# Hash attention and a maxout FFN on one core: the last third of `w_out` is loaded with the middle third, into the tiles that stage the output

## The chip, the cores and the metric

One core of a Trainium2 chip runs the whole program. The metric is device time in microseconds (us) from the start to the end of the program, the median of several runs; lower is better. A profile of a single execution gives the times inside.

## The reference

```
# q, k, v: (4, 8, 768, 64) float32   proj: (64, 6)   w1, w2, w3: (512, 768)   w_out: (768, 512)
q_bits, k_bits = (q @ proj > 0), (k @ proj > 0)      # 6 bits give a bucket for each position
mask   = bucket(q)[:, None] == bucket(k)[None, :]
scores = where(mask, (q @ k.T) / sqrt(64), -1e9)
attn   = softmax(scores)                             # per batch and head, 768 x 768
x      = (attn @ v), heads side by side              # (3072, 512)
h      = max(max(x @ w1, x @ w2), x @ w3)            # (3072, 768)
out    = h @ w_out                                   # (3072, 512)
```

## The kernel before

The work is cut by batch `b` (4), by pair of heads `pr` (4) and by half of the query positions `hf` (2). For each pair, q, k and v are loaded in float32 (`load`, L250), split on VectorE and ScalarE into two float16 parts (`split_h` L268 or L266, `split_r` L273), and turned so that the head dimension lies on the partitions. For the first six pairs TensorE turns them (`pe_T`, L292), for the others a transposing DMA from SyncE (`xbar`, L282, tile `T`). TensorE multiplies the operands with the hash matrix (`hash_mm`, L312); VectorE makes the bits, TensorE turns them, and two small DMAs bring them through DRAM into the operand's spare rows (`bit_out` L349, `bit_in` L352). A score (`score`, L395) then has the hash match in it, and `expo` (L401, ScalarE) makes the weights `AT`. `attend` (L413) multiplies them with v and sums into one PSUM tile `av`; there is a single `av` buffer, which VectorE frees by `norm_t` (L430). GpSimd sums v for the mean (`vsum`, L363 to L366), TensorE spreads it (`mean_mm`, L376), and ScalarE casts v (`vcast`, L202, tile `vone`).

When all four pairs of a half are done, `x` is turned by a DMA (`x_bar`, L457, tile `xT`) and the FFN of that half (`ffn`) is spread between the scores of the next one: `l1` (L478) multiplies by w1, w2 and w3, `l1_evac` takes the maximum (L487), `l2` (L496) multiplies by `wout_sb`, ScalarE copies the result out of PSUM into a tile `osb` (`l2_evac`, L202; pool `op`, `OSB` = 5 buffers), and SyncE stores it (`store`, L507).

The order on each engine is fixed before the program runs. `Plan.run` goes through a table of tasks with planned costs, priorities and counted buffers, and calls each task's function when the plan would start it; on the chip an engine works through its own list in that order and only waits for semaphores. So all DMAs that SyncE issues stand in one list, and an instruction that waits holds up all behind it. Each of them uses one of eight DMA semaphores in turn, so it also waits for the DMA issued eight before it.

The weights come from `weights(b, pr, parts)`. Half of `w3`, and `w_out` in three thirds, are loaded in float32 by SyncE into a staging tile `ws` (`stage_w`, L670; two buffers of 1024 elements a partition) and cast to float16 by GpSimd (`cast_w`, L204 through `copy`). A third of `w_out` is two blocks of 128 rows, 512 KB. With two `ws` buffers the third load waits until the first cast is done. The plan has a task for each load and each cast:

```
ld = add(("SP", 0.5), -60 if w == "o" else -70, [], lambda e, w=w, i=i: stage_w(w, i, e), take=("ws",),
         xfer=1.4 if w == "o" else 1.1, after=[prev])
...
parts.append(add(("POOL", 1.5 if w == "o" else 1.1), -60, [ld], lambda e, w=w, i=i: cast_w(w, i, e),
                 give=("ws",)))
```

The pair whose loads follow the first two thirds on SyncE's list is (2, 0): batch 2, pair 0. Behind them stand the transposing DMA of pair (1, 3), then the third load, then the `x_bar` of batch 0's second half.

Of the kernel before, what the change touches and what calls it, by code (L numbers as in the profile page):

```python
# [8 lines left out]
FP32 = mybir.dt.float32  # L9
# [124 lines left out]
def kernel(  # L134
# [12 lines left out]
    nc = tc.nc  # L147
    B, H, S, D = q.shape
    NBITS = proj.shape[1]
    P = 128  # L150
    NCH = S // P
    DM = H * D
# [34 lines left out]
    op = ctx.enter_context(tc.tile_pool(name="op", bufs=OSB))  # L187
# [12 lines left out]
    def copy(e, o, i):  # L200
        if e == "ACT":
            nc.scalar.copy(o, i)  # L202
        else:
            ENG[e].tensor_copy(o, i)  # L204
# [21 lines left out]
    wout_sb = konst.tile([P, NF, DM], FP16, name="wout_sb")  # L226
# [430 lines left out]
    wst_tiles = {}  # L657

    def w_view(w, i):
        c = slice(2 * i, 2 * i + 2)  # L660
        if w == "o":
            return moe_w_out.rearrange("(c p) m -> p c m", p=P)[:, c, :], wout_sb[:, c, :]
        f = slice(w[0] * DF // 2, (w[0] + 1) * DF // 2)
        return (moe_w1, moe_w2, moe_w3)[w[1]].rearrange("(c p) f -> p c f", p=P)[:, c, f], w_sb[w[1]][:, c, f]

    def stage_w(w, i, e):
        from_dram = w_view(w, i)[0]
        t = wst.tile([P, 2 * DM], FP32, tag="ws", name="ws")
        wst_tiles[w, i] = t[:, 0 : 2 * from_dram.shape[2]].rearrange("p (c f) -> p c f", c=2)
        nc.sync.dma_start(wst_tiles[w, i], from_dram)  # L670

    def cast_w(w, i, e):
        copy(e, w_view(w, i)[1], wst_tiles.pop((w, i)))

    def weights(b, pr, parts):
        if (pr or b) and parts[0] not in plain and parts[0] != "o":
            prev = add(("POOL", 0.1), -150, [bounced[b, pr]], lambda e: hold(b, pr, e), after=[wprev[0]])
        elif pr or b:
            prev = bounced[b, pr]
        else:  # L680
            prev = ready_v[0, 0]
        for w in parts:
            if w == "o" or w in plain:
                parts = []
                for i in range(NF // 2) if w == "o" else range(NJ // 2):
                    ld = add(("SP", 0.5), -60 if w == "o" else -70, [], lambda e, w=w, i=i: stage_w(w, i, e), take=("ws",),
                             xfer=1.4 if w == "o" else 1.1, after=[prev])
                    prev = ld
                    parts.append(add(("POOL", 1.5 if w == "o" else 1.1), -60, [ld], lambda e, w=w, i=i: cast_w(w, i, e),
                                     give=("ws",)))  # L690
                wload[w] = plan.join(parts, ())
                continue
            else:
                prev = add(("POOL", 0.8), -100, [], lambda e, w=w: None if w == LATE else load_w(w[1], w[0], e),
                           xfer=2.15, after=[prev])
            wload[w] = prev
        wprev[0] = prev
# [116 lines left out]
```

## Time and profile before

| what | us |
|---|---|
| median of five runs | 268.29 |
| the five runs | 265.15, 265.61, 268.29, 268.84, 268.96 |
| the profiled execution, its own time | 267.9 |
| its span, first to last instruction | 266.1 |
| TensorE busy | 256.6 (96% of the span) |
| ScalarE busy | 196.2 (74%) |
| VectorE busy | 177.0 (67%) |
| GpSimd busy | 41.8 (16%) |
| granted TensorE clock | 0.999 of full speed |

The profiled execution's own time is 1.8 us longer than its span. Times within the profile count from the span's start. In the profile's lines the columns of the timeline are start, duration, engine, line, operation, output and inputs, the count of instructions merged, and in brackets the idle time before and what ended it. SPq is SyncE's list; a DMA's duration there is the time to issue it, not to move its bytes. KB and MB are as the profile counts them.

### The profile page before, as it was taken

How to read it: one execution, taken by the hardware profiler on the slowest of the kernel's cores; microseconds unless marked ns; L12 is line 12 of the kernel's file. 1: busy time of each engine (PE TensorE's matmuls, PEld its weight loads, DVE VectorE, ACT ScalarE, POOL GpSimd, SP SyncE). 2: the span in 40 equal slices, each digit the busy share in tenths (PEclk: the TensorE clock that was granted, in tenths of full speed). 3: DMA queues.
4: the chain of work that ended last, by engine and by line, in shares of the span. 5: the costliest groups of instructions: out<-in, count | busy, mean ns of one | idle time of the engine just before them, and what ended most of it. 6: DMA issues, size and time to landing. Idle time of an engine off the chain costs nothing.

```text
span 266.1 us, 7323 instructions
## 1 busy us (share of the span) xinstructions
PE 256.6 (96%) x2992; PEld 174.8 (66%) x2992; DVE 177.0 (67%) x394; ACT 196.2 (74%) x283; POOL 41.8 (16%) x57
## 2 busy tenths in 40 slices
PE   8599999999999999999999999999999999999995
PEld 8488776767656666677666767765666656565552
DVE  4699789989857898458985795651655526345260
ACT  5589999987936889989989889898899642332422
POOL 1331056083310333003330030000000000000000
PEclk9999999999999999999999999999999999999999
DMA  6991489999997899979993997312030060120303
GB/s 188 336 288 36 137 257 268 282 229 331 228 231 244 219 274 167 221 224 205 182 286 109 217 166 132 61 22 84 36 62 0 4 173 6 42 79 0 121 0 119
DMA packets 67408, 41.69 MB, mean 157 GB/s; under 512 B 48046, under 2 KB 63662, under 8 KB 67374
## 3 DMA queue, kind: packets, MB, share of 16 engines
q1 hardware_dynamic: 64654, 39.26, 57.7%
q0 software_dynamic: 2640, 1.97, 4.8%
q8 instruction: 23, 0.38, 0.6%
q14 instruction: 11, 0.09, 0.1%
q10 hardware_dynamic: 80, 0.00, 0.0%
HBM read 25.72 MB, written 6.84 MB: 122 GB/s over the span
## 4 chain that ended last, share of the span: by engine, by line
PE 79%; DMA 9%; DVE 4%; ACT 2%; SPq 2%; POOL 1%; issue 1%; ACTq 0%; POOLq 0%
PE ps L478 32%; PE sc L395 19%; PE po L496 11%; PE av L413 10%; DMA v<-in_v_dram 2%; PE hps L312 2%; DMA q<-in_q_dram 2%; DMA dr<-bt 2%; DMA ws<-in_moe_w_dram 2%; PE tps L292 2%; ACT AT L401 2%; DVE s L273 1%; SPq L250 1%; DVE s L268 1%; PE hps L310 1%
## 5 line engine op out<-in xcount | busy, mean ns | idle before, releaser
L401 ACT ACTIVATE AT<-sc 128x768 f16<-128x768 f32 x192 | 146.2, 815 | 14.9 <-PE sc L395 12.9
L478 PE MATMUL ps<-xT,w_sb 128*128 128x384 f16 x576 | 106.3, 326 | 0.0
L395 PE MATMUL sc<-T 128*128 128x384 f16 x384 | 92.9, 325 | 1.0 <-ACT AT L401 0.4
L487 DVE TENSOR_TENSOR ht<-ht,ps 128x384 f16<-128x384 f16 x96 | 52.9, 551 | 47.1 <-PE ps L478 44.7
L413 PEld LDWEIGHTS <-AT 128*128 128x128 f16 x1152 | 59.5, 97 | 22.8 <-issue 0.2
L478 PEld LDWEIGHTS <-w_sb 128*128 128x128 f16 x576 | 52.6, 98 | 30.4 <-issue 0.5
L413 PE MATMUL av<-vone,AT 128*128 128x65 f16 x1152 | 65.5, 193 | 0.0
L395 PEld LDWEIGHTS <-T 128*128 128x128 f16 x384 | 30.3, 97 | 11.8 <-issue 1.5
L496 PE MATMUL po<-wout_sb,ht 128*128 128x512 f16 (+1 forms) x150 | 33.7, 370 | 0.0
L202 ACT CAST ht<-ps 128x384 f16<-128x384 f32 x28 | 13.4, 479 | 26.2 <-DVE ht L487 19.1
L202 ACT COPY osb<-po 128x512 f32<-128x512 f32 (+1 forms) x24 | 13.6, 568 | 18.6 <-PE po L496 18.6
L273 DVE SCALAR_TENSOR_TENSOR s<-q,s 128x384 f16<-128x384 f32 x32 | 21.8, 697 | 4.6 <-ACT s L266 4.4
L363 POOL TENSOR_TENSOR vt<-v 128x384 f32<-128x384 f32 x12 | 14.1, 1179 | 66.9 <-DMA v<-in_v_dram 66.7
L430 DVE TENSOR_TENSOR t<-av,mv 128x390 f32<-128x390 f32 x32 | 17.9, 561 | 7.9 <-PE av L413 7.8
L496 PEld LDWEIGHTS <-ht 128*128 128x128 f16 x150 | 14.1, 98 | 13.7
L449 DVE TENSOR_TENSOR xn<-t,rr 128x384 f16<-128x384 f32 x32 | 19.0, 592 | 1.1
L273 DVE SCALAR_TENSOR_TENSOR s<-k,s 128x384 f16<-128x384 f32 x32 | 18.8, 606 | 0.2
L204 DVE CAST ht<-ps 128x384 f16<-128x384 f32 x20 | 11.1, 555 | 10.5 <-PE ps L478 10.2
L292 PE MATMUL tps<-iden,s 128*128 128x128 f16 x168 | 13.7, 223 | 2.6 <-DVE bit L322 2.4
L292 PEld LDWEIGHTS <-s 128*128 128x128 f16 x168 | 11.0, 100 | 3.9 <-DVE s L273 2.7
L202 ACT CAST vone<-v 128x768 f16<-128x768 f32 x12 | 10.0, 836 | 1.4 <-DMA v<-in_v_dram 1.4
L312 PEld LDWEIGHTS <-T 128*128 128x128 f16 x336 | 10.0, 96 | 1.0
(54 smaller groups left out, 142.3 us busy)
## 6 DMA issues: line engine op xcount, KB each, us to landing
v<-in_v_dram SPq DMA_DIRECT2D x16, 384.0 KB
out_dram<-osb SPq DMA_DIRECT2D x23, 256.0 KB
q<-in_q_dram SPq DMA_DIRECT2D x15, 384.0 KB
k<-in_k_dram SPq DMA_DIRECT2D x15, 384.0 KB
w_sb<-in_moe_w_dram POOLq DMA_DIRECT2D x5, 384.0 KB, 11.6
ws<-in_moe_w_out_dram SPq DMA_DIRECT2D x3, 512.0 KB
ws<-in_moe_w_dram SPq DMA_DIRECT2D x2, 384.0 KB
dr<-bt SPq DMA_DIRECT2D x15, 36.0 KB
```

The costliest lines, as they stand in the source:

```text
L202: nc.scalar.copy(o, i)
L273: nc.vector.scalar_tensor_tensor(out=s[:, a0:a1, D : 2 * D], in0=raw_view(n, b, pr, heads), scalar=QS, in1=s[:, a0:a1, 0:D], op0=AluOp.mul ...
L292: nc.tensor.transpose(p16[:, c * P : (c + 1) * P], S16[b, pr][:, a0 + c, :], iden[:])
L312: nc.tensor.matmul(o, T[b, pr][:, a, :], PAB[:], start=True, stop=True)
L395: nc.tensor.matmul(sc[:, i, 0:HQ], t[:, NA2 + hh * NCH + 2 * j + i, :], t[:, hh * NCH + hf * CH : hh * NCH + (hf + 1) * CH, :], start=True ...
L401: nc.scalar.activation(AT[:], scs.pop(u)[:, :, 0:HQ], ActFn.Exp, bias=EXP_BIAS, scale=EXP_SCALE)
L413: nc.tensor.matmul(av[:, o : o + D + 1], AT[:, i, c * P : (c + 1) * P], vones[b % 2][:, 2 * pr + hh, 2 * j + i, 0 : D + 1], start=slot == ...
L430: nc.vector.tensor_tensor(out=t[:, :, :, 0 : D + 1], in0=av[:, :, :, 0 : D + 1], in1=mv, op=AluOp.add)
L449: nc.vector.tensor_tensor(out=xv, in0=t[:, :, :, 0:D], in1=rr[:].to_broadcast([P, 2, CH, D]), op=AluOp.mult)
L478: nc.tensor.matmul(ps[:, 0:HQ], w_sb[i][:, jc, fb * P : (fb + 1) * P], xTs[b, hf][:, jc, :], start=jc == 0, stop=jc == NJ - 1)
L487: nc.vector.tensor_tensor(out=ht[:], in0=ht[:], in1=ps[:, 0:HQ], op=AluOp.max)
L496: nc.tensor.matmul(ps[:, m0:m1], hts[b, hf, fb][:, c * P : (c + 1) * P], wout_sb[:, fb, m0:m1], start=fb == 0, stop=fb == NF - 1)
```

## The change

The last third (blocks 4 and 5 of `w_out`, 256 KB each) is no longer loaded into a `ws` tile by a task of its own. When the plan reaches the load of the middle third, `stage_w` first issues two loads into two tiles of the output staging pool `op` (tag `osb`), and then the middle third's load into `ws`. When it reaches the middle third's cast, GpSimd casts the two blocks first and then the middle third. The tasks of the last third stay in the plan with their planned costs, and emit nothing. The plan's count of free `osb` buffers is not changed by the two tiles.

```diff
     def stage_w(w, i, e):
+        if w == "o" and i == 2:
+            return
+        if w == "o" and i == 1:
+            for c in (4, 5):
+                wst_tiles[w, c] = op.tile([P, DM], FP32, tag="osb", name="osb")
+                nc.sync.dma_start(wst_tiles[w, c][:], moe_w_out[c * P : (c + 1) * P, :])
         from_dram = w_view(w, i)[0]
         t = wst.tile([P, 2 * DM], FP32, tag="ws", name="ws")
         wst_tiles[w, i] = t[:, 0 : 2 * from_dram.shape[2]].rearrange("p (c f) -> p c f", c=2)
         nc.sync.dma_start(wst_tiles[w, i], from_dram)
 
     def cast_w(w, i, e):
+        if w == "o" and i == 2:
+            return
+        if w == "o" and i == 1:
+            for c in (4, 5):
+                copy(e, wout_sb[:, c, :], wst_tiles.pop((w, c))[:])
         copy(e, w_view(w, i)[1], wst_tiles.pop((w, i)))
```

In the built program every other instruction keeps its place on its engine. On SyncE's list the two new loads stand right behind the first third's load; on GpSimd's list the two new casts stand right behind the first third's cast.

## The prediction

> **What bounds the kernel now.** I read the page's busy times first, then the waits of TensorE, then the stretch around the change engine by engine, in the timeline.
>
> ```profile
> PE 256.6 (96%) x2992; PEld 174.8 (66%) x2992; DVE 177.0 (67%) x394; ACT 196.2 (74%) x283; POOL 41.8 (16%) x57
> ```
> ```profile
> PE tps L292 <- DVE bit L322: 2.4, 1, 2.4
> PE wps L229 <- DVE ones L212: 1.1, 1, 1.1
> ...
> PE svp L376 <- POOL vsum L366: 0.3, 1, 0.3
> ```
>
> TensorE (PE) is busy for 96% of the span. In its waits (total, times, longest, us) there is no line in which L496, the product with `wout_sb`, waits for GpSimd (POOL). The windows of 2 us around the change show the same (PE busy and count, granted clock, DMA share, GB/s):
>
> ```profile
> 64.00:66.00 2.00, 2.00 (x44) 1.00 1.01 309
> ...
> 72.00:74.00 2.00, 2.00 (x28) 1.00 1.13 84
> 74.00:76.00 2.00, 2.00 (x35) 1.00 1.28 288
> ```
>
> "Busy" is not yet "without a stall", so I look at the spacing. The last third is cast at 73.92; the three groups of six products that use it are these:
>
> ```profile
> 73.92 1.04 POOL L204 CAST wout_sb<-ws 128x1024 f16<-128x1024 f32 x1 [3.45 <-DMA ws<-in_moe_w_out_dram]
> ```
> ```profile
> 74.18 1.46 PE L496 MATMUL po<-wout_sb,ht 128*128 128x512 f16 x6
> 75.47 0.75 PE L312 MATMUL hps<-PAB,T 128*128 128x12 f16 x24
> 76.07 1.46 PE L496 MATMUL po<-wout_sb,ht 128*128 128x512 f16 x6
> 77.37 0.28 PE L339 MATMUL bps<-iden,bit 128*72 128x128 f16 x2
> 77.48 1.46 PE L496 MATMUL po<-wout_sb,ht 128*128 128x512 f16 x6
> ```
>
> From the start of a group to the start of what follows: 1.29, 1.30, and 1.29 us for the third (the next product starts at 78.77). The first group, the only one that could meet a late cast, is as short as the others. Its fifth product, the first to use block 4, starts at 74.18 + 4 x 1.29/6 = 75.04; the cast ended at 73.92 + 1.04 = 74.96. So the last third came in time by 0.08 us, and in this execution the change has no stall to remove.
>
> **What it removes.** One load of 512 KB that SyncE issues late, and one cast of 1.04 us. SyncE's list (start, time to issue):
>
> ```profile
> 59.95 1.53 SPq L250 DMA_DIRECT2D q<-in_q_dram  x1
> 61.54 0.46 SPq L250 DMA_DIRECT2D k<-in_k_dram  x1
> 62.04 0.47 SPq L250 DMA_DIRECT2D v<-in_v_dram  x1
> 62.61 5.68 SPq L282 DMA_TRANSPOSE T<-s  x1
> 68.40 0.52 SPq L670 DMA_DIRECT2D ws<-in_moe_w_out_dram  x1
> 69.01 1.42 SPq L457 DMA_TRANSPOSE xT<-xn  x1
> ```
>
> The load is issued at 68.40, behind a transposing DMA of 5.68 us, and its cast starts 5.52 us later. Gone with it are 69.01 - 68.40 = 0.61 us of SyncE's list. TensorE gains nothing: 0.00 us.
>
> **What it adds and moves.** The same 512 KB is now issued at about 59.5, ahead of the loads of q, k and v of pair (2, 0), as two DMAs. Four things follow.
>
> 1. SyncE's list. The first two thirds were issued in 0.91 us together (59.00 to 59.91), some 0.48 each with the gap, so two more move q, k, v and the transposing DMA of pair (1, 3) later by 0.96 us. Before, that DMA ran from 62.61 to 68.29; it now starts at 63.57. If it still takes 5.68 it ends at 69.25. Its user is `hash_mm` at 75.47, more than 6 us on. Behind it the third load is gone, so `x_bar` goes from 69.01 to 69.35, and its xT is read first by L478 at 78.77. Cost 0. The wait for the DMA eight before adds nothing, for those are the transfers issued around 48 to 51 us.
>
> 2. The bytes. How long 512 KB keeps the DMA engines is in GpSimd's idle time, which ends as loads land:
>
> ```profile
> 63.26 1.04 POOL L204 CAST wout_sb<-ws 128x1024 f16<-128x1024 f32 x1 [3.98 <-DMA ws<-in_moe_w_out_dram]
> 64.62 1.04 POOL L204 CAST wout_sb<-ws 128x1024 f16<-128x1024 f32 x1 [0.32 <-DMA ws<-in_moe_w_out_dram]
> 67.73 1.66 POOL L363 TENSOR_TENSOR vt<-v 128x384 f32<-128x384 f32 x1 [2.08 <-DMA v<-in_v_dram]
> ```
>
> The two thirds landed 64.62 - 63.26 = 1.36 us apart; q, k and v, 1152 KB, took 67.73 - 64.62 = 3.11 us behind them, 1.04 each, which is the same 370 KB/us. So 512 KB put in front delays each of the three by 1.36 us: q from 65.66 to 67.02, k from 66.70 to 68.06, v from 67.73 to 69.09. The other end: the third load, amid transposing DMAs, needed 5.52 us from issue to cast. I take 1.36, since the new loads stand between plain loads as the rows of 1.36 do. A gain is not to be had here: moving bytes ahead makes nobody's load earlier.
>
> What each of them meets:
>
> ```profile
> 66.31 0.55 DVE L268 TENSOR_SCALAR s<-q 128x768 f16<-128x768 f32 x1
> ...
> 67.97 0.55 DVE L268 TENSOR_SCALAR s<-k 128x768 f16<-128x768 f32 x1
> 68.67 0.57 DVE L430 TENSOR_TENSOR t<-av,mv 128x390 f32<-128x390 f32 x1 [0.16 <-PE av L413]
> 69.39 0.56 DVE L487 TENSOR_TENSOR ht<-ht,ps 128x384 f16<-128x384 f16 x1 [0.15 <-PE ps L478]
> ```
>
> VectorE's split of q waits from 66.31 to 67.02, 0.71 us. Behind it on VectorE stand the bits' copy, the rest of the split, then L430, which frees the only `av` buffer, then L487, which frees a PSUM bank. The split of k is moved to 68.68, later than its load (68.06), so it adds no wait. L430 has 0.16 us of idle time ahead of it and starts 0.55 late, at 69.22, ending at 69.79; TensorE's next L413 into `av` starts at 70.10. That leaves 0.31 us. L487 ends at about 70.3; the bank it frees is due back at 72.45, three banks later in the rotation. Idle time of 1.09 us ahead of the L487 at 73.37 takes up the rest. ScalarE's cast of v starts at 69.44, later than 69.09. GpSimd's sums of v end at 71.8 in place of 70.47; the mean's product is at 73.29. All on path: 0.00 us, with the 0.31 us as the thinnest cover; what is late beyond it TensorE stands still for.
>
> 3. GpSimd's casts. The two half casts aren't in the trace; they lie between 0.46 (a sum of 128x128) and 0.9 us (the cast of 128x768), say 0.52, half of 1.04. By that the middle third is cast from 65.98, when it lands, to 67.0, and L496 needs it at 74.18. Beside a GpSimd that is busy VectorE is slower: L449 took 0.92 us at 63.79 and 0.56 at 75.48. For the split of q that is some 0.1 us (0.55 at 66.31 against 0.66 at 55.54, beside GpSimd's sums of v); it comes off the 0.31. Cost 0.
>
> 4. The `osb` buffers. The first stores are issued at 76.64, ten us after the casts have emptied the two tiles. Five buffers in turn are still five. Cost 0.
>
> The Trainium skill speaks against part 2: "DMA: Bandwidth & Descriptors", section "Anatomy of one DMA", gives each DMA a fixed cost near 2.0 us beside its bytes (measured there for DMAs issued from GpSimd), so splitting a load pays once more. By that rule, as an estimate, q, k and v would be late by 2 x 2.0 + 1.2 = 5.2 us and not 1.36, and the second rival below would come true, at some 271.8 us. The row disagrees: the second third landed 1.36 us after the first, bytes and fixed cost together. I go by the row.
>
> **Sum.** 267.9 us for the profiled execution, minus 0.0, plus 0.0: 267.9. It lies 0.4 below the median of the runs shown, 268.29, so against that median I forecast no change and name 268.2 us. Its own range is 267.0 to 269.2.
>
> **The rivals.**
>
> First, faster: the five runs fall in two groups, 265.15 and 265.61, and 268.29 to 268.96. If in the upper group the last third comes some 3 us late, the 0.08 us of cover being gone there, then TensorE stands still at 75.0, and the change puts all runs into the lower group: 265.4 us, 1.1% less. For it: the thin cover, and a load that hangs behind 5.68 us of a transposing DMA. Against it: the profiled execution, 267.9, stands nearer the upper group and has no stall there. A median that falls into the lower group by chance gives the same number.
>
> Second, slower: the load of q lands later than I say, because its place among other transfers costs more than 1.36 us. TensorE is held from a delay of 0.65 (to 66.31) + 0.16 + 0.87 (from the end of L430 at 69.23 to 70.10) = 1.68 us on. ScalarE's cast of v, with the weights of the next scores queued behind it, is held from 1.71 us on. At the far end, 5.52, TensorE loses 5.52 - 1.68 = 3.84: 272.1 us. For it: transposing DMAs share the engines, and the DMA share is at 1.0 all through. Against it: the five landings at one rate.
>
> Third, the change doesn't do what it says: the plan might reorder other work, since it keeps the tasks. The built order shows that it does not; the time would be 268.3 again, so this is within the forecast.
>
> **How the numbers follow.** Forecast, no change: 0.58. Lower group: 0.24. Late q: 0.18, of which about half lies above 270.6. About 1% is what a measurement of this kernel can tell from no change, given the two groups. So faster by over 1%: 0.24, within 1%: 0.58, slower by over 1%: 0.18. The range that holds 8 in 10 takes in the first rival and the near half of the second: 264.9 to 270.6.
>
> **What would show it.** Right: in the profile after, the three L496 groups at about 74 are still 1.3 us each, VectorE idles some 0.7 us ahead of the split of q near 66 and PE has no new wait; the casts of `wout_sb` are over by 67 and `vt` starts near 69.1. Wrong: an L413 or L395 after 68 us that waits for L430 or ScalarE; a v that lands after 69.5; or the L496 group at 74 shorter than 1.29 with a span 3 us less.

## The result and the profile after

The change makes the kernel slower by a little: ratio to before 1.0044, 95% interval 1.0025 to 1.0062. The medians are 267.47 us before (79 runs) and 268.72 us after (44 runs). The ratio is taken over the runs within 1.5% of the fastest of their kernel, the medians over all. Of 267.5 us the ratio is 1.2 us, between 0.7 and 1.7. The profiled execution of after took 269.26 us, with a span of 267.5 us.

The page's busy times are nearly those of before, and the new line stands among the costliest groups: a wait of TensorE for VectorE (idle us before the group, and who ended it).

```profile
PE 257.5 (96%) x2992; PEld 176.0 (66%) x2992; DVE 175.7 (66%) x394; ACT 196.4 (73%) x283; POOL 42.0 (16%) x58
...
L413 PE MATMUL av<-vone,AT 128*128 128x65 f16 x1152 | 65.5, 193 | 1.3 <-DVE t L430 1.3
```

The waits of the stretch from 60 to 80 us that bear on it:

```profile
DVE s L268 <- DMA q<-in_q_dram: 2.2, 1, 2.2
ACT vone L202 <- DMA v<-in_v_dram: 1.5, 1, 1.5
...
PE av L413 <- DVE t L430: 0.9, 1, 0.9
```

In the timeline of after, first VectorE, then TensorE:

```profile
68.78 0.56 DVE L268 TENSOR_SCALAR s<-q 128x768 f16<-128x768 f32 x1 [2.19 <-DMA q<-in_q_dram]
...
70.39 0.55 DVE L268 TENSOR_SCALAR s<-k 128x768 f16<-128x768 f32 x1
70.86 0.56 DVE L430 TENSOR_TENSOR t<-av,mv 128x390 f32<-128x390 f32 x1
```
```profile
69.72 0.81 PE L478 MATMUL ps<-xT,w_sb 128*128 128x384 f16 x4
71.47 0.34 PE L413 MATMUL av<-vone,AT 128*128 128x65 f16 x6 [0.94 <-DVE t L430]
...
75.82 1.46 PE L496 MATMUL po<-wout_sb,ht 128*128 128x512 f16 x6
77.12 0.75 PE L312 MATMUL hps<-PAB,T 128*128 128x12 f16 x24
```

VectorE idles 2.19 us for q of pair (2, 0). The splits stand ahead of L430, L430 ends at 71.42, and TensorE's L413 starts at 71.47, 0.05 us behind it. So L430 ended the wait. ScalarE waits too, 1.5 us for v; how little that can have cost stands with theory V below. This is the second rival of the prediction. The first group of L496 takes 77.12 - 75.82 = 1.30 us, as before: the early cast bought nothing. GpSimd and SyncE:

```profile
64.79 1.04 POOL L204 CAST wout_sb<-ws 128x1024 f16<-128x1024 f32 x1 [5.25 <-DMA ws<-in_moe_w_out_dram]
65.77 1.17 POOL L204 CAST wout_sb<-osb 128x512 f16<-128x512 f32 x2
67.42 1.04 POOL L204 CAST wout_sb<-ws 128x1024 f16<-128x1024 f32 x1 [0.47 <-DMA ws<-in_moe_w_out_dram]
71.30 1.02 POOL L363 TENSOR_TENSOR vt<-v 128x384 f32<-128x384 f32 x1 [2.84 <-DMA v<-in_v_dram]
```
```profile
61.00 1.71 SPq L676 DMA_DIRECT2D ws<-in_moe_w_out_dram  x1
62.76 0.47 SPq L250 DMA_DIRECT2D q<-in_q_dram  x1
...
64.36 7.58 SPq L282 DMA_TRANSPOSE T<-s  x1
72.04 2.61 SPq L457 DMA_TRANSPOSE xT<-xn  x1
```

A second loss is at the end. SyncE asks there for its eight DMA semaphores, one after the other. The line gives the count of such instructions (ten, for two more follow the eight questions), their durations, and when the first and the last of them started; first before, then after:

```profile
L809 SPq EVENT_SEMAPHORE  x10: 17/28/28, 263.8 to 266.1; - x10
```
```profile
L820 SPq EVENT_SEMAPHORE  x10: 17/28/28, 266.2 to 267.4; - x10
```

Before, the first question passes at 263.8, right behind the last store's issue; the eighth passes at 265.2, when the last store has landed. After, the first one is passed only at 266.2, when the last store has landed, and the other seven follow it. By the semaphore updates in the trace, the span ends 0.93 us after the last landing before, and 1.33 us after it in the changed kernel.

To compare executions whose starts differ, I count time from one product on TensorE: the mean's L376 at 57.29 before and at 57.43 after. TensorE before, then the mark after:

```profile
57.29 0.22 PE L376 MATMUL svp<-vsum,ones 128*128 128x130 f16 x1 [0.27 <-POOL vsum L366]
...
70.10 0.35 PE L413 MATMUL av<-vone,AT 128*128 128x65 f16 x6
```
```profile
57.43 0.22 PE L376 MATMUL svp<-vsum,ones 128*128 128x130 f16 x1
```

From this mark to the L413 that stands behind L430 it is 12.81 us before and 14.04 us after: 1.23 us lost.

### The profile page after: what moved, and what is told of

It is laid out like the page before. It is cut to its first block, busy times and chain, and to the rows that moved or that the text cites. A ratio compares the mean times of both kernels' runs of the same rounds, so it can differ in the third digit from the quotient of the medians.

```text
span 267.5 us, 7326 instructions
## 1 busy us (share of the span) xinstructions
PE 257.5 (96%) x2992; PEld 176.0 (66%) x2992; DVE 175.7 (66%) x394; ACT 196.4 (73%) x283; POOL 42.0 (16%) x58
## 4 chain that ended last, share of the span: by engine, by line
PE 82%; DMA 6%; DVE 4%; ACT 2%; SPq 2%; POOL 1%; issue 1%; ACTq 0%; POOLq 0%
PE ps L478 32%; PE sc L395 20%; PE po L496 12%; PE av L413 11%; DMA q<-in_q_dram 6%; PE hps L312 3%; PE tps L292 2%; ACT AT L401 2%; DVE s L273 1%; DVE xn L449 1%; SPq L676 1%; SPq L250 1%; PE hps L310 1%; PE svp L373 1%; DVE s L268 1%
## 5 line engine op out<-in xcount | busy, mean ns | idle before, releaser
L413 PEld LDWEIGHTS <-AT 128*128 128x128 f16 x1152 | 59.5, 97 | 24.3 <-issue 1.7
L413 PE MATMUL av<-vone,AT 128*128 128x65 f16 x1152 | 65.5, 193 | 1.3 <-DVE t L430 1.3
L496 PE MATMUL po<-wout_sb,ht 128*128 128x512 f16 (+1 forms) x150 | 33.6, 370 | 0.0
L363 POOL TENSOR_TENSOR vt<-v 128x384 f32<-128x384 f32 x12 | 13.3, 1106 | 67.7 <-DMA v<-in_v_dram 67.5
L430 DVE TENSOR_TENSOR t<-av,mv 128x390 f32<-128x390 f32 x32 | 17.9, 560 | 8.0 <-PE av L413 8.0
L496 PEld LDWEIGHTS <-ht 128*128 128x128 f16 x150 | 14.1, 98 | 13.7
L273 DVE SCALAR_TENSOR_TENSOR s<-q,s 128x384 f16<-128x384 f32 x32 | 20.2, 645 | 4.2 <-ACT s L266 4.0
L449 DVE TENSOR_TENSOR xn<-t,rr 128x384 f16<-128x384 f32 x32 | 20.1, 627 | 1.1
L292 PE MATMUL tps<-iden,s 128*128 128x128 f16 x168 | 15.0, 235 | 1.8 <-DVE bit L322 1.8
L292 PEld LDWEIGHTS <-s 128*128 128x128 f16 x168 | 11.9, 106 | 2.8 <-DVE s L273 1.8
```

The costliest lines, as they stand in the source:

```text
L273: nc.vector.scalar_tensor_tensor(out=s[:, a0:a1, D : 2 * D], in0=raw_view(n, b, pr, heads), scalar=QS, in1=s[:, a0:a1, 0:D], op0=AluOp.mul ...
L292: nc.tensor.transpose(p16[:, c * P : (c + 1) * P], S16[b, pr][:, a0 + c, :], iden[:])
L413: nc.tensor.matmul(av[:, o : o + D + 1], AT[:, i, c * P : (c + 1) * P], vones[b % 2][:, 2 * pr + hh, 2 * j + i, 0 : D + 1], start=slot == ...
L430: nc.vector.tensor_tensor(out=t[:, :, :, 0 : D + 1], in0=av[:, :, :, 0 : D + 1], in1=mv, op=AluOp.add)
L449: nc.vector.tensor_tensor(out=xv, in0=t[:, :, :, 0:D], in1=rr[:].to_broadcast([P, 2, CH, D]), op=AluOp.mult)
L496: nc.tensor.matmul(ps[:, m0:m1], hts[b, hf, fb][:, c * P : (c + 1) * P], wout_sb[:, fb, m0:m1], start=fb == 0, stop=fb == NF - 1)
```

## The experiments

Theory P: the bytes ahead of pair (2, 0)'s loads make q late; VectorE waits, and with it L430 and TensorE. Theory S: the staging costs (half loads, half casts, shared tiles). Theory L: the bytes hold the transposing DMA of (1, 3) and what stands behind it. Theory V: ScalarE's cast of the late v. Theory E: the end, by the count of DMAs. In all these kernels TensorE, VectorE and ScalarE run the same instructions in the same order as before.

**The halves at the old place** (e1_halves_late, e1b_halves_late):

```diff
+    def third():
+        for c in (4, 5):
+            wst_tiles["o", c] = op.tile([P, DM], FP32, tag="osb", name="osb")
+            nc.sync.dma_start(wst_tiles["o", c][:], moe_w_out[c * P : (c + 1) * P, :])
     def stage_w(w, i, e):
+        if w == "o" and i == 2:
+            return third()
...
```

> The third goes in two half loads into the output staging tiles, but at its old place behind the transposing DMA of pair (1, 3); everything else is as before. Theory P (place: the 512 KB ahead of pair (2, 0)'s loads hold VectorE's split of q, and so L430 and TensorE): q is as early as before, no idle time ahead of the split of q at 66, no L413 that waits for L430 near 70, and the time of before, 267.5 us, ratio 1.000. Theory S (staging: the half loads, the half casts or the shared output tiles cost the time): the loss of the changed kernel stays, ratio near 1.004.

> The halves at the old place once more, since its first ratio, 1.0035 with an interval from 0.9997 to 1.0073, left it open. Theory P: 1.000, and no L413 waits for L430 near 70. Theory S (half loads, half casts, shared tiles): 1.004.

Measured: 1.0035 (0.9997 to 1.0073) and 1.0019 (0.9981 to 1.0058); the times leave a loss of some tenths of a per cent open. Both intervals hold 1.000 as well as 1.004. In neither profile does VectorE wait for q or L413 for L430: the L413 comes 12.82 us after the mark in both. What they share with the changed kernel is the end: 1.33 and 1.34 us from the last landing. So the staging does not make the stall.

**The halves behind v of (2, 0)** (e2_behind_v), and **between k and v** (e5_behind_k); both have `third()` and cast at the old place:

```diff
     def load(n, b, pr, heads, e):
...
+        if (n, b, pr) == ("v", 2, 0):   # "k" in e5_behind_k
+            third()
...
```

> The same two half loads stand right behind the load of v of pair (2, 0), ahead of the transposing DMA; the casts are at the old place. Theory P: q, k and v of (2, 0) land as before, so VectorE's split of q starts near 66.3 without idle time, no L413 waits for L430, ratio 1.000 (0.997 if the early third is worth anything). Theory S: ratio near 1.004. Theory L (late followers: the transposing DMA and what stands behind it are held by the bytes, and that is what costs): TensorE still stalls by about 1 us after 70, ratio near 1.004.

> The two half loads stand between the loads of k and of v of pair (2, 0); the casts are at the old place. So q and k land as before and only v is late. Theory P (it is VectorE's split of q that holds TensorE): no idle time ahead of the split of q, no L413 that waits for L430; ScalarE's cast of v may idle 0 to 1 us and TensorE lose up to 0.5 us, ratio 1.000 to 1.002. Theory V (ScalarE's cast of the late v holds the weights of the next scores, and would do so alone): ScalarE idles 1.5 us ahead of the cast of v as in the changed kernel, and the ratio is near 1.004.

Measured: behind v 1.0069 (1.0032 to 1.0105), between k and v 1.0031 (0.9998 to 1.0064). Neither P's 1.000 nor its profile came true for the first: q was late although nothing had been put ahead of it.

```profile
67.05 0.56 DVE L270 TENSOR_SCALAR s<-q 128x768 f16<-128x768 f32 x1 [1.77 <-DMA q<-in_q_dram]
```
```profile
69.74 0.34 PE L415 MATMUL av<-vone,AT 128*128 128x65 f16 x6 [0.53 <-DVE t L432]
```

In that execution the first third of `w_out`, which stands in the same place as ever, had the first of its sixteen semaphore updates at 60.95, the fifteenth at 61.34 and the last at 64.70, and the loads behind it trailed likewise. The stall needs a late q, and the bytes are not the only way to one.

Between k and v neither VectorE nor TensorE waits for q. Its time fits P and V alike. Nor does ScalarE wait for v there, so this run does not test V. (Its L415 is 0.63 us late all the same, at 13.44 us after the mark: most of it is a wait for the bits at 64.50, behind a VectorE product of 1.44 us beside GpSimd's cast.) What V can have cost is read from the kernels where ScalarE did wait for v. In the changed kernel, 1.5 us, TensorE is 1.23 us late at L413 and 1.51 at the mean's product behind it (74.94), so at most 0.28 more. With double bytes and in e9_seven_more, 2.4 and 2.0 us, TensorE is as late at that product, 2.44 and 2.07 us, as at L413. So V is not the main cost; whether it would cost alone is not shown.

**Double the bytes** (e3_double):

```diff
+            for c in (4, 5):
+                more = op.tile([P, DM], FP32, tag="osb", name="osb")
+                nc.sync.dma_start(more[:], moe_w_out[c * P : (c + 1) * P, :])
```

> The changed kernel with another 512 KB, two more loads into two more output tiles that nobody reads, at the same place. Theory P: q lands another 1.3 to 1.5 us later and the issue moves by another 1 us, so VectorE idles 3.5 to 4.7 us ahead of the split of q (2.2 in the changed kernel), L413 waits for L430 by 1 us plus 1.3 to 2.5, and the ratio to before is 1.009 to 1.014. Theory S: two more loads without casts add less than 0.5 us, ratio 1.004 to 1.006.

Measured: 1.010 (1.0062 to 1.0139), inside P's range and beyond S's. VectorE idles 3.40 us ahead of the split of q, a little under P's 3.5, and L413 waits 2.25 us for L430, at the lower end of P's 2.3 to 3.5.

```profile
71.91 0.34 PE L413 MATMUL av<-vone,AT 128*128 128x65 f16 x6 [2.25 <-DVE t L430]
```

**Pair (2, 0) first** in the changed kernel (e6_pair_first) and in the kernel before (e7_pair_first_late):

```diff
     def stage_w(w, i, e):
+        if w == "o" and i == 0:
+            for n in "qkv":
+                do_load(n, 2, 0, (0, 2), e)
+                first_pair.append((n, 2, 0))
...
```

> The changed kernel, with the loads of q, k and v of pair (2, 0) issued ahead of all three thirds of w_out; the bytes ahead of the transposing DMA of pair (1, 3) are the same as in the changed kernel. Theory P (the late q of (2, 0) holds VectorE, L430 and TensorE): q lands some 2.7 us earlier than before, no idle time on VectorE ahead of the split of q, no L413 that waits for L430 near 70, ratio to before 0.998 to 1.001. Theory L (the bytes hold the transposing DMA of (1, 3) and all that stands behind it on SyncE's list, and that is what costs): that DMA still ends its issue near 72 and its T lands near 75, TensorE stalls later, between 75 and 100, ratio near 1.004 to 1.007.

> The kernel before, with the loads of q, k and v of pair (2, 0) issued ahead of the first two thirds of w_out; the last third stays late, behind the transposing DMA. Theory P: q has 2.7 us more of slack, so a slow transfer can't hold VectorE here, ratio 0.998 to 1.000. Theory L: as before, ratio 1.000. If it is above 1.003, the order of these loads costs something that neither theory has.

Measured: 1.0013 (0.9968 to 1.0059) and 1.0039 (1.0005 to 1.0073). The first interval holds the changed kernel's 1.0044 too, so the time does not show that the loss is gone; the profile shows that the wait is. The second lies above both theories. The wait at L413 for L430 is gone in both; theory L's late T is there (in the first, its issue ends at 70.03 and it landed at 73.6) and no hash product waits for it. But each has a new wait. In the first, GpSimd's sums of v now stand behind all casts:

```profile
73.24 0.22 PE L382 MATMUL svp<-vsum,ones 128*128 128x130 f16 x1 [0.99 <-POOL vsum L372]
```

In the second all of `w_out` is later, and the last third's cast comes too late: the stall that an early last third removes (in the first of the two this group is whole and takes 1.29 us).

```profile
73.88 1.02 PE L502 MATMUL po<-wout_sb,ht 128*128 128x512 f16 x4
75.19 0.59 PE L502 MATMUL po<-wout_sb,ht 128*128 128x512 f16 x2 [0.29 <-POOL wout_sb L204]
```

It cost 0.3 to 0.45 us here. Two products with w1 to w3 (L484 here), at 57.47 and 61.30, wait for VectorE's maximum (L493) and come some 0.4 and 0.5 us late. Both come before the first load that the edit moves has landed (62.22): up to 55.55 VectorE had idled 1.38 us for the q of an earlier pair.

**More executions, and the end** (after_again, before_again; e8_one_more, e9_seven_more). The last two add loads of 8 KB ahead of the last four stores, one to the kernel before, seven to the changed one:

```diff
+        if (b, hf, c) == (B - 1, 0, CH - 1):
+            for n in range(7):          # 1 in e8_one_more
+                few = konst.tile([P, 16], FP32, name=f"few{n}")
+                nc.sync.dma_start(few[:], moe_w_out[0:P, 0:16])
```

> The changed kernel, one more look at where TensorE stalls between 57 and 110 us. Theory P: VectorE idles 1 to 2.5 us ahead of the split of q near 66 and an L413 waits for L430 by 0 to 1.2 us near 70, as in the first profile; the amount moves with how late the transfers run. If there is no such wait here, the first profile's stall was an accident.

> The kernel before, one more look. Theory P: no idle time on VectorE ahead of the split of q near 66, or at most 0.5 us where the transfers run late, and no L413 that waits for L430 near 70; from the last landing to the end 0.93 us. A stall of 0.5 us or more at L413 here would say that the kernel before pays it too, and that it is not the change's.

> The kernel before, with one more load of 8 KB that nobody reads, issued by SyncE ahead of the last four stores. Theory E (the end: one more DMA moves every later one to the next of the eight DMA semaphores, so the last store is on the first that SyncE asks for at the end and the seven other questions, some 0.06 us each, come after its landing): from the last store's landing to the end of the span 1.32 us as in the changed kernel, 0.93 in the kernel before. If the end is 0.93 here, the longer end comes from the staging in the output tiles and not from the count of DMAs.

> The changed kernel, with seven more loads of 8 KB that nobody reads ahead of the last four stores, so that there are eight more DMAs than before and the last store is on the eighth semaphore again. Theory E: from the last landing to the end 0.93 us, as before the change, in place of 1.32. The stall near 70 is not touched by this: VectorE idles 0.5 to 2.2 us ahead of the split of q, L413 waits for L430 by 0 to 1.2 us.

Measured, one execution each: 266.81, 265.08, 267.93 and 267.20 us. The changed kernel's second execution has a late q and no wait at L413; its 0.51 us of idle time is under the 1 to 2.5 that were expected. The third, with seven more loads far behind it, has the longest waits of the three, 3.06 and 1.90 us, and both lie above what was expected. VectorE in these two, then TensorE in the third:

```profile
66.06 0.56 DVE L268 TENSOR_SCALAR s<-q 128x768 f16<-128x768 f32 x1 [0.51 <-DMA q<-in_q_dram]
```
```profile
67.27 0.56 DVE L268 TENSOR_SCALAR s<-q 128x768 f16<-128x768 f32 x1 [3.06 <-DMA q<-in_q_dram]
```
```profile
69.96 0.34 PE L413 MATMUL av<-vone,AT 128*128 128x65 f16 x6 [1.90 <-DVE t L430]
```

The kernel before, profiled again, alone and with the one load added, shows no wait for q; alone:

```profile
64.30 0.55 DVE L268 TENSOR_SCALAR s<-q 128x768 f16<-128x768 f32 x1
```

Theory E came true both ways. With one more DMA the first question at the end waits until 264.8, though the last store was issued by 263.3, and the end comes 1.38 us after the landing. With eight more than before it is 0.93 us again, in the changed kernel. The lines, one more and then eight:

```profile
L813 SPq EVENT_SEMAPHORE  x10: 17/28/28, 264.8 to 266.1; - x10
```
```profile
L824 SPq EVENT_SEMAPHORE  x10: 17/28/28, 263.2 to 265.4; - x10
```

In all, five executions whose last store is on the last semaphore have 0.91 to 0.93 us, and eight with one DMA more than before have 1.32 to 1.38. The kernel with double bytes has three more, its last store is on the third semaphore, and it has 1.23: five questions behind the landing in place of seven. So 0.4 us of the loss comes with every execution, by the count of DMAs and not by where `w_out` is loaded.

**A version meant to keep the early third without its costs** (e10_all_early): pair (2, 0) first, the sums of v ahead of the middle and last casts, seven more loads.

```diff
     def cast_w(w, i, e):
+        if w == "o" and i == 1:
+            return
+        if w == "o" and i == 2:
+            copy(e, w_view(w, 1)[1], wst_tiles.pop((w, 1)))
+            for c in (4, 5):
+                copy(e, wout_sb[:, c, :], wst_tiles.pop((w, c))[:])
+            return
...
```

> A version that keeps the early last third without its two costs: q, k and v of pair (2, 0) are issued ahead of w_out, all three thirds stand behind them, GpSimd sums v ahead of the casts of the middle and last third, and seven loads of 8 KB that nobody reads put the last store back on the eighth semaphore. By theories P and E: no L413 waiting for L430 near 70, no mean's product waiting for GpSimd near 73 (1.15 us in the version without the moved sums), end 0.93 us, ratio to before 0.998 to 1.001. If T of (1, 3) lands later than its hash product at 75, a new wait of up to 1 us stands there and the ratio is up to 1.004.

Measured: 1.0025 (0.9994 to 1.0057), no gain. The end is 0.93 us and the mean's product at 73 no longer waits, but L413 waits 0.39 us at 70.85, with q in time. VectorE and GpSimd:

```profile
67.23 2.36 DVE L279 SCALAR_TENSOR_TENSOR s<-q,s 128x384 f16<-128x384 f32 x2
```
```profile
66.82 1.07 POOL L204 CAST wout_sb<-ws 128x1024 f16<-128x1024 f32 x1 [5.94 <-DMA ws<-in_moe_w_out_dram]
67.85 1.32 POOL L369 TENSOR_TENSOR vt<-v 128x384 f32<-128x384 f32 x1
```

The two halves of the split that take 1.01 us in the kernel before (67.03) take 2.36 us here, beside GpSimd's cast and sum, and L430 is late by that. The Trainium skill, "GPSIMD Engine Reference", section "Key points", has GpSimd share its way into SBUF with VectorE and names contention with VectorE instructions that have two inputs there, as these have; the page gives no size, and here it is 1.35 us in two instructions. No version that beats both kernels came out of this.

## Why the prediction was wrong

The 268.2 us that I named lie within 0.6 of the 268.72 measured, and inside the range, by luck: they stand for no change from the median of five runs, 268.29, and the median of 79 is 267.47. The two groups of those five were chance too: 53 of the 79 runs lie between them. I also held 1% to be what a measurement can tell; with this many runs it is 0.2%, and the loss of 0.44% is clear of that. My own sign of being wrong came true: an L413 that waits for L430, and a v that landed after 69.5 (at 71.23).

*The bound, and what it removes.* Right. The three groups of L496 are as long as before, 1.30 us, and the early third gained nothing. The first rival, a stall at 75 in the kernel before, did not show in three executions of it (one with the 8 KB load at the end).

*SyncE's list.* Half right. I moved q, k, v and the transposing DMA by 0.96 us; it was 1.6. Before, q's issue was itself the slow one, 1.53 us, and ended 61.48 - 57.29 = 4.19 us after the mark; after, the load ahead of it took 1.71, and q's issue ended at 63.23 - 57.43 = 5.80. The transposing DMA took 7.58 us and not 5.68. In all fourteen profiles its issue ended 0.6 to 0.8 us after the last plain load ahead of it had landed, so I read it as following the bytes, not its own time. As predicted, its T had enough slack: no hash product waited.

*The bytes: the step that failed.* The step took q's landing as one time, 1.36 us later than before, and set that against a threshold of 1.68. The 1.36 was read from two loads that landed one after the other in one execution. The trace has sixteen semaphore updates for each load, as many as there are DMA engines, so I read them as one for each engine. After the mark, q's first and last update come at (us):

| kernel | first | last | split of q starts | L413 late by it, from 10.05 | L413 late, measured |
|---|---|---|---|---|---|
| before | 7.09 | 8.26 | 9.02 | 0 | 0 |
| before, second execution | 7.34 | 8.23 | 8.96 | 0 | 0 |
| before, one more load at the end | 7.93 | 8.57 | 9.21 | 0 | 0.16 |
| halves at the old place | 6.76 | 9.00 | 9.02 | 0 | 0.01 |
| the same, second run | 6.98 | 8.90 | 8.97 | 0 | 0.01 |
| halves between k and v | 7.77 | 8.97 | 9.69 | 0 | 0.63 |
| halves behind v | 7.31 | 10.78 | 10.80 | 0.75 | 0.68 |
| after | 9.20 | 11.33 | 11.35 | 1.30 | 1.23 |
| after, second execution | 8.47 | 9.92 | 9.94 | 0 | 0.29 |
| after, seven more loads at the end | 8.72 | 12.18 | 12.20 | 2.15 | 2.08 |
| double bytes | 10.18 | 12.54 | 12.56 | 2.51 | 2.44 |

The first updates went from 7.45 on average in the three executions of before to 8.80 in the three of after: 1.35 us, the term as sized. But VectorE starts when the last update is in (0.02 us behind it in the rows where it waits), and that went from 8.35 to 11.14: 2.79 us. Part of this can be chance. In the first seven rows, with nothing put ahead of q, first and last update lie 0.6 to 3.5 us apart, and in the three of after 1.4 to 3.5, so that the bytes widen this spread is not shown. Over those seven rows the last update is at 8.96 on average, and the step from there is 2.2 us. In after itself the first third of `w_out`, in its old place, was already spread over 1.91 us, from 62.83 to 64.74.

So q is late by 1.7 to 3.9 us against its 8.26 in the profile of before, not by 1.36, and the threshold, 1.68, lies at the lower end of that. v, for which I had 1.36 too, landed 13.80 us after the mark against 10.37, 3.4 later. Without the bytes a late q held TensorE in one of seven executions, with them in three of four. The two half loads are no worse than one: in after the first updates of the loads ahead of q come at 5.40, 6.06 and 6.75 us after the mark, 0.66 and 0.69 apart, and that of the next, of 512 KB, at 8.09, 1.34 on.

The Trainium skill's fixed 2.0 us for each DMA ("DMA: Bandwidth & Descriptors", section "Anatomy of one DMA"), which the page has for DMAs that GpSimd issues, does not add up in this queue of SyncE's: the updates stand 0.66 and 0.69 us apart.

*The threshold.* Right, and closely. The split of q may start 9.02 us after the mark and TensorE is held from 9.02 + 0.16 + 0.87 = 10.05 on. The last two columns agree within 0.1 us wherever L413 waits for L430. The second execution of after has its 0.29 from an earlier wait for bits, at 65.61. What I had as a cover of 0.31 us was real, and smaller than the spread of the load that was to stay under it. The two landings that gave 1.36 trailed by the same 1.19 us, so the lag fell out of their difference; with no spread on the term I gave this rival 0.18.

*The last transfers.* Missed. I wrote that the wait for the DMA eight before adds nothing, and did not follow the semaphores to the end: with one DMA more the last store moves on from the eighth semaphore to the first, 0.4 us.

*The sum.* At L413 TensorE was late by 1.23, 0.29 (not by q) and 2.08 us in three executions, a mean of 1.2. Less is left at the end: from the mark to the issue of the last store it is 206.14, 205.33 and 205.82 us in the executions before, 205.8 on average, and 206.49, 205.54 and 207.72 us after, 206.6, so 0.8 us remain. With 0.4 at the end that is 1.2 us, as the ratio says. Three of each carry the 0.8 only roughly: in the kernels of the experiments where no late q holds L413 the same stretch takes 205.7 to 207.2 us. How often the stall comes, and what makes an engine trail in a given run, stays open.

## What to carry to other kernels

Where TensorE runs an order fixed ahead, moving a load forward moves every load behind it, and the first engine that waits for one of those holds what stands behind it in its own list: ask what the next load's user is holding up, not only whether the moved load is early enough. Size a delay by when the last DMA engine is done, with its spread over several executions, and compare it with the thinnest cover; a cover thinner than the spread is a cost in some of the runs. A change in the number of DMAs can move the end by itself, here by 0.4 us.

## What the runs showed of the hardware that I had not expected

The last of a load's sixteen updates can come 3.5 us behind the first: 8.72 and 12.18 in the changed kernel with seven more loads, 7.31 and 10.78 in the kernel with the halves behind v, where nothing was put ahead of q. The lag can stay over several loads in a row: 1.19, 1.19 and 1.18 us for two thirds of `w_out` and q before, 1.91, 1.91, 1.88 and 1.84 us for the four loads ahead of q after.

In every execution one packet of 16 KB, in the queue that the profile calls instruction, runs in this stretch. It took 0.95 to 1.39 us in the three executions of before and the three of after, and 2.68 us in the kernel with the halves behind v, whose first third trailed by 3.75 us. In the two runs with the halves at the old place the load that landed before this packet was over is spread over 0.4 and 0.6 us, and the next over 2.2 and 1.9, though the packet took 0.88 and 1.09 us. That it makes an engine trail is not shown: it took 0.95 us where q's updates spread over 0.9 us, and 1.27 us where they spread over 3.5.

Asking for a semaphore that has long been reached costs SyncE 0.06 us at the end, and seven such questions behind the last landing are 0.4 us. Beside GpSimd's cast and sum, in one execution, VectorE's second step of the split took more than double: 2.36 against 1.01 us for two.
